# A gated mix of attention and SwiGLU on one core: GpSimd takes strips of any width, the gate's operand is made earlier, and the order table is another

## The chip, the core and the metric

The kernel runs on one core of a Trainium2 chip. The core has TensorE (matrix products, PE in the profile; its weight loads are PEld), VectorE (DVE), ScalarE (ACT) and GpSimd (POOL), and SyncE (SP), which here only issues DMAs. Matrix products go to PSUM, from where VectorE or ScalarE take them to SBUF. The metric is the device time of one execution in microseconds, as a median of several runs.

## What is computed

```python
x = A_x                                   # 2048 rows of 512, bf16
g = _sigmoid((x * gate_w).sum(-1, keepdims=True))
a = _A_ref(x, A_wqkv, A_wo)               # attention, 32 heads of 16
b = _B_ref(x, B_w_gate, B_w_up, B_w_down) # (silu(x @ w_gate) * (x @ w_up)) @ w_down, width 1792
return g * a + (1 - g) * b
```

In the attention, scores are `q k^T / 4`, the softmax runs over all 2048 keys, and its result times `v` goes through the projection `wo`. The largest part of the work is the softmax's exponentials: 32 heads x 2048 queries x 2048 keys.

## The kernel before

**Units.** Heads are taken four at a time (8 groups), queries 512 at a time (4 blocks). A pair of group and query block is a *unit*; there are 32, taken in a fixed order (`UNIT`). A unit has 16 blocks of 128 keys. For each block of keys TensorE makes scores for four heads (four tiles of 128 x 512 in PSUM), an engine takes the exponential, and TensorE multiplies the result with the values and adds it into the unit's output `o_ps`. A column of ones in the values gives the denominators. When all blocks of a unit are in, an output copy (`post`) takes `o_ps` to `osb`.

**Two ways to the exponential.** Scores that ScalarE handles go two heads at a time to `s_t` (128 x 1024 in PSUM, two buffers), and one `Exp` of ScalarE writes `e_t`; a block of keys is two such instructions. Scores that VectorE handles go one head at a time to `d_t` (128 x 512 in PSUM, three banks, shared with all other products). VectorE scales and shifts each into a 16-bit integer whose bits are a bf16 near the exponential; four of them fill a buffer of 128 x 2048 (`c_t`, or space of `kaug` or `wd_t`: NS = 7 buffers in all). The accuracy comes from a mean over shifted versions. With `groups[n] == 4`, three more *copies* are made, each the buffer plus a constant (`SHIFTS`), and TensorE multiplies all four with the values. With `groups[n] == 2`, two bit-masked copies are made and one of them becomes the *product* of the buffer with it; TensorE multiplies two versions. Copies and products are objects of class `Pass` in the list `vops`. They read and write SBUF alone.

**GpSimd's part.** GpSimd can't take PSUM here; it takes passes from VectorE: shifting copies (of groups of four) as two halves of 1024 columns (`g_half`, `GHALF`), and of products up to a few pieces of 448 columns off the end (`piece`, `G_COLS`), the rest being done by VectorE (`product`). `claim` chooses the pass, and `g_now` gives it to GpSimd if VectorE has PSUM reads ahead (`d_wait`, `owed`) that last about as long as the strip. `beside` makes the strip wait for VectorE's last SBUF operation. In the plan, `plan.lock` keeps VectorE from SBUF operations until the strip ends; on the chip no wait stands for that, only the order of the instructions on VectorE.

**The order.** The whole program is put in order by a planner in the kernel's Python: it keeps a clock per engine (`plan.pe`, `plan.dve`, `plan.act`, `plan.pool`) with a fixed cost for each kind of instruction, and decides step by step what TensorE does next (a pair of score tiles, a value product, a piece of a chain of another product) and what VectorE does next (`fill_dve`). Every instruction is chained to the one before on its engine, so the order on the engines is the planner's. `v_unit` and `v_take` decide which blocks of keys go to VectorE; `quad` whether as group of four or two. The string `TURNS` has two characters for each pair of score tiles, which change single decisions there: `turn_of` (for instance `s`: no chain piece now; `d`: no `d_t` now) and `way_of` (for instance `t`: GpSimd takes no products; `q`: a strip may end later; `n`: no strip; `f`, `g`: kind of group). A dot changes nothing.

**Around it.** The remaining products run as chains of pieces with deadlines (`Pacer`): projections, the feed-forward part (`gu`, tanh on ScalarE, `dps`, `ops`), and the normalisation. Three places matter here. `gate_end` computes the gate from `ge`, and `turn_odds`, some thirty us later in the profile, transposes it by a product with an fp32 copy `rd` of the identity, made on VectorE at the head of `turn_odds`. Unit 0 begins with a provisional bound; `q0_again` lets ScalarE compute a `ratio`, and `parts` multiplies it in by a product `rp` on TensorE. At the end, four output tiles `a_l_a`, `a_l_b`, `al`, `al_o` collect the last projection (`last_pieces` for the first two, `tail` one matmul at a time for the others), the last output copy on ScalarE gives denominators (`dt`), their reciprocals `rt` are spread by `rps`, and the last matmul of each tile follows.

Of the kernel before, what the change touches and what calls it, by code (L numbers as in the profile page):

```python
# [53 lines left out]
class Pacer:  # L54
# [33 lines left out]
    "..............h.............d...............h.............j..n....b.h.........k....ns........x.."  # L88
    ".......................y.n.......m..........s..............w......s..x........d.....b.kg...f...."
    ".........fbt....bt..b.........a.................o.......s.........s...h.dx....o................."  # L90
    "........bve..m.........wk...............s.......h.dx......i..q....h.............s...c...s......."
    "....k..g...l....o................................v.....x.f..............o.............s..v...f.."
    "................c......g..a...h..l...l...wey...wh..y....j...c....t..k...s........f....en....b..."
    "d...................a.....c......f.......................m........k..............g........c....."
    "...f...........v......dx......................sl.v.......v..j..............q..........b........."
    "..j.................s.........i.........hf.......g............................................o."
    ".............g......................h...............................................b..........."
    ".....l................................................c............x...........................g"
    "..i...i..m..e.....hm.....we.....a..xel.......v.f........o.............................h........."
    "...g..........d.s..mc.......h............................................m......................"  # L100
    ".............................................g............d......................x............s."
    "............a..v..................b.....................k"
# [4 lines left out]
def kernel(  # L107
# [771 lines left out]
    class Pass:  # L879


        def __init__(self, cost, key, n, ready, home, k, h, y):
            self.cost, self.key, self.n, self.ready, self.home = cost, key, n, ready, home
            self.k, self.h, self.y = k, h, y
            self.halves, self.c, self.left = [0, 1], None, NV * QBW

        def run(self, engine, cols=slice(0, NV * QBW), t=None):

            n, k, y = self.n, self.k, self.y
            if not self.home:  # L890
                product(n, self.h, y, self.left)
                return None
# [12 lines left out]
        def done(self, t):  # L905

            n, k, (h, c) = self.n, self.k, self.c
# [14 lines left out]
            if not todo[n]:  # L922
                vops.insert(0, Pass(MUL_US, None, n, late.pop(n) + PRODUCT_LAG, False, None, self.h, self.y))

# [12 lines left out]
    PRODUCT_LAG = 0.0  # L937
    late = {}
    todo = {}
    gq = []  # L940
    GHALF = NV * QBW // 2

    def g_half(engine, start=0.0):

        g = gq[0]
        half = g.halves.pop(0)
        ins = g.run(engine, slice(half * GHALF, (half + 1) * GHALF))
        if engine is gps:
            beside(ins)
            t = plan.pool = plan.lock = start + G_US  # L950
        else:
            t = plan.dve
        if not g.halves:
            gq.pop(0)
            g.done(t)

# [6 lines left out]
    G_US = 1.06  # L963
    G_COLS, GP_US = 448, 1.05
    G_KEEP = 2
    G_OVER = 0.1

    def claim(now):

        if gq:  # L970
            return gq[0]
        front = [v for v in vops if v.n == vops[0].n and v.poolable()] if vops else []
        if front and not front[-1].home and (front[-1].left < G_KEEP * G_COLS or way_of(pairs[0]) == "t"):
            return None
        if front and front[-1].home and min(c_free) > now + 0.05:
            return None
        return front[-1] if front and front[0].n // KT <= closed + AHEAD else None

    def g_now(now):

        while True:
            g = claim(now)
            if g is None:
                return
            start = max(plan.pool, plan.alone + 0.17, g.ready + 0.17, 0.0 if g.c is not None or not g.home else min(c_free) + 0.1)
            t = now
            for ready, cost in sorted([(d[0], 0.6) for d in d_wait] + [(o[0], o[1]) for o in owed if not wide(o[1])]):
                if ready > t + 0.05:
                    break
# [3 lines left out]
            if not g.home:  # L993
                g.piece(start)
                continue
            if not gq:
                vops.remove(g)
                gq.append(g)
            g_half(gps, start)

    def g_dve():
        if gq[0].c is None:
            plan.dve = max(plan.dve, min(c_free))
        spend_v(0.335, plan.lock)
        g_half(vec)
        took()

    def product(n, h, y, left):
        i, c = part.pop(n)
        cols = slice(0, left)  # L1010
        vec.tensor_tensor(out=c[:, cols].bitcast(BF16), in0=y[:, cols].bitcast(BF16), in1=c[:, cols].bitcast(BF16), op=ALU.mult)
        ready(n, 1, i, c)
        drop(h, plan.dve + 0.2)
        y_live[0] -= 1

    def c_ready():
        return min(c_free) if not vops or vops[0].home else vops[0].ready
# [6 lines left out]
    def pay_v():  # L1024
        v = vops.pop(0)
        spend_v(v.cost, max(plan.lock, v.ready), v.key)
        v.run(vec)
        if v.home:
            v.done(plan.dve)
        took()  # L1030

    def fill_dve():

        code = way_of(pairs[0])
        while plan.dve <= plan.pe + 0.2:
# [6 lines left out]
            fit = bool(vops) and not shut and vops[0].n // KT <= closed + AHEAD and c_ready() <= now  # L1042
# [14 lines left out]
            elif gq and not shut and gq[0].n // KT <= closed + AHEAD and (gq[0].c is not None or min(c_free) <= now):  # L1057
                g_dve()
            elif d_wait or owed or vops and vops[0].n // KT <= closed + AHEAD:
                t = min([w[0] for w in d_wait] + [max(o[0], plan.lock if wide(o[1]) else 0.0) for o in owed[:1]]  # L1060
                        + [max(c_ready(), plan.lock)] * bool(vops and vops[0].n // KT <= closed + AHEAD))
# [83 lines left out]
    def post(un):  # L1145
# [5 lines left out]
        elif un == UNITS - 1:  # L1151
            act(out=osbs[un][:, :], in_=o_of.pop(un)[:, :], func=ACT.Identity, bias=tiny[:, 0:1], scale=1.0)
# [192 lines left out]
    def q0_again(p):  # L1345
# [12 lines left out]
    def scale_part(p):  # L1358
        def f():
# [11 lines left out]
                     cond=lambda: part_done and ratio_done)  # L1371
# [228 lines left out]
    def next_pv():  # L1600
        flush_act()
        while not pv_list(None):
# [4 lines left out]
            elif gq and (gq[0].c is not None or min(c_free) < 1e9):  # L1607
                g_dve()
# [56 lines left out]
    GQL = lambda: [v for v in vops + gq if v.poolable()]  # L1665
# [77 lines left out]
    while closed < UNITS or vops or vcur or gq:  # L1743
# [26 lines left out]
    assert not vops and not gq and not vready and not vcur and not d_wait and not copies and au == closed == UNITS  # L1770
# [5 lines left out]
    tail(2)  # L1776
# [4 lines left out]
    tail(2)  # L1781
# [51 lines left out]
```

## Time and profile before

| | us |
|---|---|
| median of 3 runs | 750.89 (750.66 to 751.36) |
| the profiled execution | 751.05 |
| its span, first to last instruction | 749.1 |
| busy: TensorE, VectorE, ScalarE, GpSimd | 725.0, 726.5, 732.7, 228.3 |
| exponentials on ScalarE, 758 | 708.2 |
| reads of `d_t` on VectorE, 532 | 349.2 |
| first exponential starts, last one ends | 13.1, 740.6 |

A row of a group reads: line, engine, operation, output <- input with shape and type, count | busy us, mean ns of one | idle us before them and what ended it. Instructions overlap, so a mean is longer than the distance between starts. The helper that chains all instructions is line 191 for TensorE, 194 for ScalarE and 203 for the others; rows are told apart by their tiles. The 349.2 are the sum of the rows of `c_t`, `kaug` and `wd_t` out of `d_t` (296.3, 50.2 and 2.7).

### The profile page before, as it was taken

The numbers are of one execution on the slowest core, as the hardware profiler recorded it, in microseconds if no ns is written. First come the engines' busy times: TensorE is split into PE (matmuls) and PEld (weight loads), VectorE is DVE, ScalarE is ACT, GpSimd is POOL, SyncE is SP. The second block draws the span as 40 slices with busy tenths as digits, with TensorE's granted clock in tenths as the row PEclk, the third lists the DMA queues.
The fourth block names the chain that finished last, engine by engine and source line by source line (L and its number), as shares of the span: only waits on it lengthen the run. The fifth ranks groups of instructions, "written<-read, shape, count | busy, mean of one in ns | idle before, by whom it ended". The sixth has DMA issues, their size and how long they took to land.

```text
span 749.1 us, 22678 instructions
## 1 busy us (share of the span) xinstructions
PE 725.0 (97%) x9180; PEld 214.4 (29%) x9181; DVE 726.5 (97%) x1222; ACT 732.7 (98%) x827; POOL 228.3 (30%) x235
## 2 busy tenths in 40 slices
PE   8999999999999999999999999999999999999997
PEld 3322222223222222222222222222222222222222
DVE  6799999999999999999999999999999999999995
ACT  5999999999999999999999999999999999999996
POOL 5024323232232224242413142333232233243410
PEclk9999999999999999999999999999999999999999
DMA  8002303144210022221100231211000322100001
GB/s 197 2 1 55 74 12 73 36 123 90 59 34 13 17 52 68 61 48 30 38 19 19 52 83 35 65 35 43 17 16 27 76 68 55 34 21 12 15 29 36
DMA packets 91025, 34.43 MB, mean 46 GB/s; under 512 B 75488, under 2 KB 90472, under 8 KB 90920
## 3 DMA queue, kind: packets, MB, share of 16 engines
q1 hardware_dynamic: 89192, 32.66, 18.2%
q8 instruction: 71, 1.16, 0.6%
q10 hardware_dynamic: 1728, 0.33, 0.2%
q14 instruction: 34, 0.28, 0.1%
HBM read 21.55 MB, written 2.35 MB: 32 GB/s over the span
## 4 chain that ended last, share of the span: by engine, by line
PE 52%; ACT 31%; DVE 10%; issue 7%; ACTq 0%; DVEq 0%
ACT e_t L194 29%; PE s_t L191 17%; PE o_ps L191 15%; PE gu L191 8%; DVE c_t L203 6%; PE ops L191 6%; ACT th L194 1%; PE qp L191 1%; PE kp L191 1%; DVE mt L203 1%; PE dps L191 1%; PE vp L191 1%; PE warm L191 1%; DVE kaug L203 1%; PE d_t L191 1%
## 5 line engine op out<-in xcount | busy, mean ns | idle before, releaser
L194 ACT ACTIVATE e_t<-s_t 128x1024 bf16<-128x1024 f32 x758 | 708.2, 1087 | 2.6 <-PE s_t L191 1.4
L203 DVE TENSOR_SCALAR c_t<-d_t 128x512 uint16<-128x512 f32 x452 | 296.3, 685 | 2.1 <-PE d_t L191 1.8
L191 PE MATMUL s_t<-qx,kaug 32*128 32x512 bf16 (+1 forms) x1192 | 231.9, 384 | 9.7 <-ACT e_t L194 8.6
L191 PEld LDWEIGHTS <-kaug 32*128 32x128 bf16 (+1 forms) x2048 | 81.3, 91 | 313.2 <-issue 309.9
L203 POOL TENSOR_SCALAR c_t<-c_t 128x1024 uint16<-128x1024 uint16 x98 | 102.3, 1044 | 171.7 <-DVE c_t L203 112.7
L191 PE MATMUL d_t<-qx,kaug 32*128 32x512 bf16 x440 | 153.7, 383 | 0.0
L191 PE MATMUL o_ps<-e_t,vaug 128*32 128x512 bf16 (+2 forms) x1560 | 147.6, 380 | 0.1
L203 DVE TENSOR_SCALAR c_t<-c_t 128x2048 uint16<-128x2048 uint16 x184 | 124.3, 687 | 1.1 <-DVE c_t L203 0.5
L191 PE MATMUL o_ps<-c_t,vaug 128*32 128x512 bf16 (+2 forms) x1416 | 123.5, 369 | 0.7 <-DVE osb L203 0.5
L203 POOL TENSOR_TENSOR c_t<-c_t 128x448 bf16<-128x448 bf16 x53 | 54.2, 1034 | 173.3 <-DVE c_t L203 114.2
L191 PEld LDWEIGHTS <-vaug 128*32 128x32 bf16 x3184 | 68.5, 95 | 102.2 <-issue 88.8
L191 PE MATMUL gu<-xT,wg 128*32 128x512 bf16 x896 | 73.2, 384 | 0.0
L191 PE MATMUL gu<-xT,wu 128*32 128x512 bf16 x896 | 67.8, 382 | 0.0
L191 PE MATMUL ops<-wd_t,mt 128*32 128x512 bf16 x672 | 57.7, 382 | 0.0
L203 DVE TENSOR_TENSOR c_t<-c_t 128x1600 bf16<-128x1600 bf16 (+3 forms) x56 | 55.9, 998 | 0.0
L203 DVE TENSOR_SCALAR kaug<-d_t 128x512 uint16<-128x512 f32 x76 | 50.2, 684 | 0.2 <-PE d_t L191 0.2
L191 PE MATMUL s_t<-q,kaug 64*128 64x512 bf16 (+1 forms) x192 | 37.4, 385 | 2.8 <-ACT e_t L194 2.7
L203 DVE SCALAR_TENSOR_TENSOR mt<-gs,gu 128x512 bf16<-128x512 bf16 x56 | 38.2, 683 | 1.1
L203 DVE SCALAR_TENSOR_TENSOR gs<-th,gu 128x512 bf16<-128x512 bf16 x56 | 38.2, 682 | 0.1
L194 ACT ACTIVATE th<-gu 128x512 bf16<-128x512 f32 x56 | 37.4, 667 | 0.0
L203 POOL TENSOR_SCALAR kaug<-c_t 128x1024 uint16<-128x1024 uint16 x18 | 18.8, 1044 | 53.8 <-DVE c_t L203 42.9
L191 PEld LDWEIGHTS <-mt 128*32 128x32 bf16 (+1 forms) x1037 | 24.6, 95 | 29.1 <-issue 22.7
(148 smaller groups left out, 533.8 us busy)
## 6 DMA issues: line engine op xcount, KB each, us to landing
wg<-in_B_w_gate_dram SPq DMA_DIRECT2D x56, 128.0 KB
wu<-in_B_w_up_dram SPq DMA_DIRECT2D x56, 128.0 KB
on<-osb SPq DMA_DIRECT2D x120, 16.0 KB
rb<-rr SPq DMA_DIRECT2D x15, 128.0 KB
wd_t<-in_B_w_down_dram SPq DMA_DIRECT2D x7, 256.0 KB
qx<-qst SPq DMA_DIRECT2D x96, 16.0 KB
qx<-aq SPq DMA_DIRECT2D x96, 16.0 KB
out_dram<-o_t SPq DMA_DIRECT2D x12, 128.0 KB
```

What stands on the lines that cost most here:

```text
L191: return ordered(nc.tensor.matmul(*args, **kw))
L194: ordered(nc.scalar.activation(*args, **kw))
L203: return lambda *a, **kw: ordered(f(*a, **kw))
```

## The change

- A pass is no longer given to GpSimd in halves or pieces of 448. `strip` computes how many columns fit into the time that is left beside VectorE's PSUM reads, with a fixed part and a price per column (`G_FIX`, `G_COPY`, `G_PRODUCT`), rounds down to a multiple of 32, takes at least 192 columns and leaves either none or at least 160. VectorE does what is left of the pass, and may be left nothing. A strip is planned to start 0.10 us after VectorE's last SBUF operation instead of 0.17, and to end at most 0.05 us (was 0.1) after VectorE's PSUM reads.
- `claim` looks through the passes of the first block of keys that GpSimd can help with; two new characters (`r`, `u`) change whether VectorE takes masked copies or others first, and whether it leaves those to GpSimd.
- The fp32 identity is made in `gate_end`; `turn_odds` uses it.
- The product with `ratio` waits in the plan until ScalarE is done with it.
- The last output copy is split into halves of 256 columns, on VectorE and ScalarE.
- The matmuls of the last projection are given one at a time, where TensorE would wait for an exponential and no value product is ready, instead of three at one place.
- `TURNS` is another string (1456 characters, 1400 before).

Counted in the two programs: 756 exponentials (758 before), 536 reads of `d_t` (532), on VectorE 262 copies and 75 products (255 and 76), on GpSimd 246 copies and 81 products (138 and 72).

```diff
 TURNS = (
...
-        later(0.5, end, plan.act + 0.05)
+            rd = work.tile([P, QBW], BF16, tag="rd", name="rd")[:, :].bitcast(F32)
+            vec.tensor_copy(out=rd[:, 0:P], in_=ident[:, :])
+            odds_rows.append(rd)
+        later(1.7, end, plan.act + 0.05)
 
     def turn_odds():
-        rd = work.tile([P, QBW], BF16, tag="rd", name="rd")[:, :].bitcast(F32)
-        vec.tensor_copy(out=rd[:, 0:P], in_=ident[:, :])
+        rd = odds_rows.pop()
...
-        def piece(self, start):
-            cols = slice(self.left - G_COLS, self.left)
-            h, c = part[self.n]
-            beside(gps.tensor_tensor(out=c[:, cols].bitcast(BF16), in0=self.y[:, cols].bitcast(BF16),
-                                     in1=c[:, cols].bitcast(BF16), op=ALU.mult))
-            plan.pool = plan.lock = start + GP_US
-            self.left -= G_COLS
-            self.cost = 0.06 + (MUL_US - 0.06) * self.left / (NV * QBW)
+        def strip(self, start, us):
+            rate = G_COPY if self.home else G_PRODUCT
+            w = int((us - G_FIX) / rate) // 32 * 32
+            if self.left - w < G_LEAVE:
+                w = self.left if w >= self.left else self.left - G_LEAVE
+            if w < G_LEAST:
+                return False
+            beside(self.run(gps, slice(self.left - w, self.left)))
+            plan.pool = plan.lock = start + G_FIX + rate * w
+            self.left -= w
+            self.cost = 0.066 + ((0.6 if self.home else MUL_US) - 0.066) * self.left / (NV * QBW)
+            if not self.left:
+                vops.remove(self)
+                self.done(plan.pool)
+            return True
...
-    G_US = 1.06
-    G_COLS, GP_US = 448, 1.05
-    G_KEEP = 2
-    G_OVER = 0.1
+    G_FIX, G_COPY, G_PRODUCT = 0.195, 0.00083, 0.00187
+    G_LEAST, G_LEAVE = 192, 160
+    G_OVER = 0.05
+    MASKS = False
...
-            start = max(plan.pool, plan.alone + 0.17, g.ready + 0.17, 0.0 if g.c is not None or not g.home else min(c_free) + 0.1)
+            start = max(plan.pool, plan.alone + 0.1, g.ready + 0.1, 0.0 if g.c is not None or not g.home else min(c_free) + 0.1)
...
-            if t == now or t < start + (G_US if g.home else GP_US) - (G_OVER if way_of(pairs[0]) != "q" else 0.4):
+            if t == now or not g.strip(start, t + (G_OVER if way_of(pairs[0]) != "q" else 0.4) - start):
                 return
...
+            if vops and vops[0].poolable() and (code == "r") != MASKS:
+                j = next((j for j, v in enumerate(vops) if not v.poolable() and v.n // KT <= closed + AHEAD), 0)
+                vops.insert(0, vops.pop(j))
...
-            act(out=osbs[un][:, :], in_=o_of.pop(un)[:, :], func=ACT.Identity, bias=tiny[:, 0:1], scale=1.0)
+            o, hw = o_of.pop(un), QBW // 2
+            vec.tensor_scalar(out=osbs[un][:, 0:hw], in0=o[:, 0:hw], scalar1=tiny[:, 0:1], scalar2=None, op0=ALU.add)
+            act(out=osbs[un][:, hw:], in_=o[:, hw:], func=ACT.Identity, bias=tiny[:, 0:1], scale=1.0)
...
-            ratio_done.append(0)
+            ratio_done.append(plan.act + 0.1)
...
-                     cond=lambda: part_done and ratio_done)
+                     cond=lambda: part_done and ratio_done and ratio_done[0] <= plan.pe)
...
-            tail(3)
+        if len(a_ps) > 2 and not pv_list(plan.pe) and not vops and len(rest) > 1:
+            n = closed * KT + done_a[closed]
+            if plan.pe + 0.22 < max(e_end.get(b, 0.0) for b in range(4 * n, 4 * n + 4)):
+                tail(1)
+                spend("F", 1)
+                continue
```

More of the change, by code (lines that the diff above doesn't have):

```diff
@@ L87 @@
 TURNS = (
[L88 to L97, printed above, removed]
@@ L884, in __init__, with run @@
             self.k, self.h, self.y = k, h, y
-            self.halves, self.c, self.left = [0, 1], None, NV * QBW
-        def run(self, engine, cols=slice(0, NV * QBW), t=None):
+            self.c, self.left = None, NV * QBW
+        def run(self, engine, cols):
             n, k, y = self.n, self.k, self.y
             if not self.home:
-                product(n, self.h, y, self.left)
-                return None
+                c = part[n][1]
+                return engine.tensor_tensor(out=c[:, cols].bitcast(BF16), in0=y[:, cols].bitcast(BF16),
+                                            in1=c[:, cols].bitcast(BF16), op=ALU.mult)
             if self.c is None:
@@ L905, in done @@
         def done(self, t):
-            n, k, (h, c) = self.n, self.k, self.c
+            n, k = self.n, self.k
+            if not self.home:
+                i, c = part.pop(n)
+                copies[n, 1] = (c.bitcast(BF16), i)
+                usable(t + 0.3, n, 1)
+                drop(self.h, t + 0.2)
+                y_live[0] -= 1
+                return
+            h, c = self.c
             todo[n] -= 1
@@ L922, in done @@
             if not todo[n]:
-                vops.insert(0, Pass(MUL_US, None, n, late.pop(n) + PRODUCT_LAG, False, None, self.h, self.y))
+                vops.insert(0, Pass(MUL_US, None, n, late.pop(n), False, None, self.h, self.y))
         def poolable(self):
             return not self.home or groups[self.n] == 4
-        def piece(self, start):
-            cols = slice(self.left - G_COLS, self.left)
-            h, c = part[self.n]
-            beside(gps.tensor_tensor(out=c[:, cols].bitcast(BF16), in0=self.y[:, cols].bitcast(BF16),
-                                     in1=c[:, cols].bitcast(BF16), op=ALU.mult))
-            plan.pool = plan.lock = start + GP_US
-            self.left -= G_COLS
-            self.cost = 0.06 + (MUL_US - 0.06) * self.left / (NV * QBW)
-    PRODUCT_LAG = 0.0
+        def strip(self, start, us):
[13 more added lines that the diff above has]
+            return True
     late = {}
     todo = {}
[L940 to L955, printed above, removed]
     def beside(ins):
@@ L961, in beside @@
                               reason="beside reads of PSUM")
-    G_US = 1.06
-    G_COLS, GP_US = 448, 1.05
-    G_KEEP = 2
-    G_OVER = 0.1
+    G_FIX, G_COPY, G_PRODUCT = 0.195, 0.00083, 0.00187
+    G_LEAST, G_LEAVE = 192, 160
+    G_OVER = 0.05
+    MASKS = False
     def claim(now):
[L970 to L977, printed above, removed]
+        first = next((v.n for v in vops if v.poolable() and v.n // KT <= closed + AHEAD), None)
+        front = [v for v in vops if v.n == first and v.poolable() and (v.c is not None or not v.home or min(c_free) <= now + 0.05)]
+        if way_of(pairs[0]) == "t":
+            front = [v for v in front if v.home]
+        begun = [v for v in front if v.left < NV * QBW]
+        return (begun or front or [None])[-1]
     def g_now(now):
@@ L990, in g_now @@
                 t += cost
-            if t == now or t < start + (G_US if g.home else GP_US) - (G_OVER if way_of(pairs[0]) != "q" else 0.4):
+            if t == now or not g.strip(start, t + (G_OVER if way_of(pairs[0]) != "q" else 0.4) - start):
                 return
[L993 to L1014, printed above, removed]
     def c_ready():
-        return min(c_free) if not vops or vops[0].home else vops[0].ready
+        return min(c_free) if not vops or vops[0].home and vops[0].c is None else vops[0].ready
     def pay_d():
@@ L1664 @@
     EAGER = lambda q, b: q == 0 and b <= 4
-    GQL = lambda: [v for v in vops + gq if v.poolable()]
+    GQL = lambda: [v for v in vops if v.home and v.poolable()]
     back = [0]
@@ L1742 @@
     flush_act()
-    while closed < UNITS or vops or vcur or gq:
+    while closed < UNITS or vops or vcur:
         fill_dve()
@@ L1769 @@
         pay()
-    assert not vops and not gq and not vready and not vcur and not d_wait and not copies and au == closed == UNITS
+    assert not vops and not vready and not vcur and not d_wait and not copies and au == closed == UNITS
     assert not at
@@ L1775 @@
     osb = osbs[un]
-    tail(2)
+    tail(min(2, len(rest)))
     dt = m_tile("dt")
```

38 lines of the change are left out of this document (22 added, 16 removed).

## The prediction

> **What bounds the kernel now.** I read the busy line of the page first, then the costly groups, then the waits, then the timeline around single stalls.
>
> ```profile
> PE 725.0 (97%) x9180; PEld 214.4 (29%) x9181; DVE 726.5 (97%) x1222; ACT 732.7 (98%) x827; POOL 228.3 (30%) x235
> ...
> L194 ACT ACTIVATE e_t<-s_t 128x1024 bf16<-128x1024 f32 x758 | 708.2, 1087 | 2.6 <-PE s_t L191 1.4
> L203 DVE TENSOR_SCALAR c_t<-d_t 128x512 uint16<-128x512 f32 x452 | 296.3, 685 | 2.1 <-PE d_t L191 1.8
> ```
>
> Three engines are busy 97 to 98%, so the average decides nothing. Idle is 16 to 24 us each, nearly all before 40 us and after 740 us; in the middle, the table by stretches has this:
>
> ```profile
> 200.00:300.00 100.00, 96.92 (x1243) 27.59 (x1235) 99.18 (x162) 99.04 (x112) 31.26 (x30) 1.00 0.16 40
> 500.00:600.00 100.00, 99.75 (x1299) 28.03 (x1297) 99.72 (x164) 100.00 (x113) 32.39 (x32) 1.00 0.14 34
> ```
>
> (Columns after the length: PE, PEld, DVE, ACT, POOL, clock, DMA share, GB/s.) So I count steps from start to start. ScalarE:
>
> ```profile
> 727.67 12.95 ACT L194 ACTIVATE e_t<-s_t 128x1024 bf16<-128x1024 f32 x14
> 118.38 0.62 ACT L194 ACTIVATE th<-gu 128x512 bf16<-128x512 f32 x1
> 118.86 6.56 ACT L194 ACTIVATE e_t<-s_t 128x1024 bf16<-128x1024 f32 x7
> ```
>
> Fourteen exponentials: (12.95 - 1.087) / 13 = 0.9125 us a step; a tanh 118.86 - 118.38 = 0.48. From the first exponential (13.11) to the end of the last (740.61) are 727.5 us. 758 x 0.9125 + 56 x 0.48 + 0.6 (two small ones) + 0.2 (the last one's end) = 719.4. ScalarE loses 8.1 us there, mostly in slips too short to show as idle. VectorE, by the same method (0.60 a step for a 512-column PSUM read or a 2048-column copy: 221.05 to 221.65; 1.13 for a whole product: 221.65 to 222.78), has 669.9 us of work between the first and the 31st output copy (at 44.5 and 721.5, 677.0 us), each instruction that stands between them at its step; ScalarE has 669.3 for the score tiles and gates issued there. These two are the bound, equally. TensorE has about 645 by the steps below, and waits for ScalarE (11.9 us in the table of waits).
>
> **The change part by part.** The two programs were counted instruction by instruction.
>
> Exponentials 758 to 756: one more block of keys goes to VectorE (a block is two exponentials, or four reads of d_t with what follows). ScalarE: -2 x 0.9125 = -1.83 us, on the path.
>
> VectorE: d_t reads 532 to 536, +2.4 us. Copies 255 with 520,192 columns become 262 with 492,960. The by-form rows give 687 ns at 2048 columns and 422 at 1024, 0.259 ns a column; less the overlap of 0.09 the rest is 0.07 an instruction: +0.5 - 7.0 = -6.5. Products 76 with 123,392 columns become 75 with 118,432; rows 1219 ns at 2048, 986 at 1600, 751 at 1152 give 0.523 a column: -2.7. Sum -6.8 us of 670, one of the two bounds.
>
> GpSimd: 138 copies of 1024 columns (1.044) and 72 products of 448 (1.034), 218.5 us, become 246 copies with 172,640 columns and 81 products with 39,264. The trace has one width of each, so the fixed part of a strip is not in it. Lower bound: the small memset's 0.10 (128x4), 274 us in all; upper: the 128x128 select's 0.29, 287 us. The planner's new 0.195 lies between and reproduces both known widths (0.195 + 0.85 = 1.045; 0.195 + 0.838 = 1.033); I take it: 280 us, so POOL's busy time goes to about 290 (284 to 297). GpSimd itself stays far from full. What it costs is on VectorE, and is bounded next.
>
> Strips against VectorE's SBUF work. The planner now assumes a strip to start 0.10 after VectorE's last SBUF operation (0.17 before), and fills VectorE's stretch of PSUM reads up to 0.05 beyond its end. Of about 160 strips that began right behind such an operation, 54 started 0.07 to 0.09 after its recorded end, 103 at 0.13 to 0.19, and a recorded end is itself some 0.09 after the next start. So strips will end about 0.08 later against the plan than now. Does that hold VectorE? Two rows:
>
> ```profile
> 331.14 1.05 POOL L203 TENSOR_SCALAR c_t<-c_t 128x1024 uint16<-128x1024 uint16 x1 [1.68 <-PE d_t L191]
> 332.06 0.69 DVE L203 TENSOR_SCALAR c_t<-c_t 128x2048 uint16<-128x2048 uint16 x1
> ...
> 199.98 2.17 POOL L203 TENSOR_SCALAR c_t<-c_t 128x1024 uint16<-128x1024 uint16 x2 [2.63 <-DVE c_t L203]
> 201.51 0.72 DVE L203 CAST rd<-ident 128x128 f32<-128x128 bf16 x1
> ```
>
> The copy at 332.06 starts 0.13 before the strip's end and takes its usual 0.69; 48 operations start 0.02 to 0.13 early and none is stretched. The cast at 201.51, 0.64 before the end, lasts until just after it: 0.72, for 128 columns. So an overlap up to 0.13 is free and a long one is held. The new overlap should be about 0.10 to 0.21. Lower bound of the cost: 0. Upper: half of 327 strips (48 of 210 now, but strips cut to a single 0.60 read will more often be followed by a copy) x 0.08 = 13 us on VectorE. I take 4, nearer the free rows, which leaves VectorE -6.8 + 4 = -2.8, still no worse than ScalarE's -1.8. The Trainium skill, SBUF — State Buffer, section "SBUF: two separate sides", says that the port pair shared by VectorE and GpSimd is an exclusive lock held for the whole instruction. By that rule every overlap would cost its length and the cost would be the upper bound or more; the cast agrees, the 48 rows do not up to 0.13.
>
> TensorE: two score rounds fewer, two 512-column rounds more (one value product, one filler), and 16 more switches between row and column tiling. From the chain (score step 0.32, then 0.33 for the first column group and 0.22 for each further) two switches cost 0.65 - 2 x 0.217 = 0.22: 8 x 0.22 = +1.7 us. I take nothing of it, since 11.9 us of waits for ScalarE cover it; uncovered, it is 1.7.
>
> The gate's fp32 operand. Now:
>
> ```profile
> 202.28 0.28 PE L191 MATMUL odds_p<-rd,odds 128*16 128x128 f32 x1 [1.17 <-DVE rd L203]
> 203.31 1.94 ACT L194 ACTIVATE e_t<-s_t 128x1024 bf16<-128x1024 f32 x2 [0.81 <-PE d_t L191]
> ```
>
> TensorE stands 1.17 for the cast that the strip held; the score tiles behind it are late and ScalarE idles 0.81. With the cast made some thirty us earlier this goes: -0.81. The cast itself stays on VectorE, at 0.2 to 0.7, in the 4 above.
>
> The ratio's condition. In the waits TensorE stands 1.03 us for ScalarE's ratio at 31.7; the exponentials there start at 31.48 and 32.74, 1.26 apart where 0.91 is usual: -0.35. Late next could be the deadline of that chain; its result is wanted only by the first output copy at 44.5.
>
> The end. The last output copy in halves on two engines: ScalarE 687 ns at 512 columns and 1087 at 1024 is 0.78 a column, 0.49 for 256; VectorE, with 742 at 512, is taken to need no longer for its half; -0.20. Now three matmuls of the last projection stand between the last score tile and the last two value products; the new order puts three column groups of another chain and four row matmuls there (0.65 + 0.43 + 0.1 against 0.65 + 0.75 now, with the same last score), so the last products can follow the exponential: -0.45. The three matmuls are made behind the reciprocals instead: 3 x 0.217 = +0.65. Together 0.0; I take 0, with -0.5 and +0.7 as ends.
>
> Sum: -1.83 - 0.81 - 0.35 + 0.0 = -3.0. The profiled execution has a span of 749.1 and a time of 751.05 (1.95 around it), 0.16 above the median of the three runs. Span 746.1, time 748.05; against the median 747.9.
>
> **The rivals.** (a) Slower: the strips hold VectorE. If the free overlap ends at 0.13 and half the strips overrun by 0.06, VectorE pays 160 x 0.06 = 9.6, net +2.8, and as the other bound it carries the end: 753.7. It decides from 6.8 / 327 = 0.021 us a strip on, where the relief is eaten. For it: two thirds of the strips start late already; a pair of strips takes 2.17, 0.08 more than two singles, which the plan leaves out. Against it: the 48 rows. (b) Faster still: of ScalarE's 8.1 us of slips 1.2 is accounted for above. If the other 6.9 comes from tiles that VectorE returns late, and 6.8 us less work there halves it, the time is 747.9 - 3.4 = 744.5. Against it: the taken 4 us of holds, and more dependences across three engines. (c) No change: TensorE paces. The chain gives it 52% and ScalarE 31%; then +1.7 stands against the -1.16 of the two stalls and the exponentials gain nothing: 750.9 + 0.5 = 751.4. Against it: its 645 us of steps to 670.
>
> **How the numbers follow.** My forecast has 0.51 (its own range 746.3 to 749.4), (b) 0.15, (c) 0.14, (a) 0.20. A difference of 0.2%, 1.5 us, is about what a measurement can tell. Faster, below 749.4: 0.51 + 0.15 = 0.66; within: 0.14; slower, above 752.4: 0.20. Range: from (b)'s value to most of (a)'s, 744.3 to 753.2, which leaves out some 0.04 below and 0.12 above.
>
> **What would show it.** Right: 756 exponentials at 0.91 to 0.93 a step, the wait of odds_p and that of rp gone, VectorE's busy time some 3 to 7 us lower, POOL near 290. Strips of 416 columns at 0.54 confirm the price; at 0.60 the fixed part is nearer 0.29 and the holds grow. Wrong by (a): 2048-column copies or narrow remainders on VectorE with means well over 687 ns, and more ScalarE idle in the middle. Wrong by (c): ScalarE's idle or mean step grows while TensorE has no waits for it.

## The result, and the profile after

| | before | after |
|---|---|---|
| median, us | 751.12 (750.34 to 751.99) | 754.48 (753.69 to 754.78) |
| profiled execution, its span | 751.05, 749.1 | 753.96, 752.2 |
| up to the first output copy | 44.5 | 42.8 |
| from there to the 31st output copy | 677.0 | 682.3 |
| from there to the end | 27.5 | 27.1 |

The ratio is 1.0042, with an interval of 1.0029 to 1.0055: slower by 0.42%, where 747.9 us was forecast. The three stretches of the span say where: the start gained 1.7 us, the end 0.4, and the middle, 30 units of the same work, lost 5.3. Of the start's 1.7 only 1.5 lie behind the first exponential; when that one starts differs by up to 1.1 us between executions of one order (12.6 to 13.7 in the runs below).

The page's busy line and two of its costly groups, after the change:

```profile
PE 731.6 (97%) x9213; PEld 215.6 (29%) x9213; DVE 728.6 (97%) x1233; ACT 733.4 (98%) x825; POOL 291.9 (39%) x352
...
L195 ACT ACTIVATE e_t<-s_t 128x1024 bf16<-128x1024 f32 x756 | 707.7, 1071 | 4.5 <-PE d_t L192 1.7
L204 DVE TENSOR_SCALAR c_t<-d_t 128x512 uint16<-128x512 f32 x460 | 299.7, 679 | 2.1 <-PE d_t L192 1.8
```

VectorE was to have 6.8 us less work, 2.8 us less with the holds that I allowed for. It is busy 2.1 us longer (726.5 before). TensorE, with 33 instructions more, is busy 6.6 us longer, and the exponentials' mean has fallen from 1087 to 1071: steps are shorter than recorded durations, so these hold some overlap with the instruction ahead, and I read a lower mean as score tiles that come too late for it.

The groups of VectorE with shapes kept apart, before and then after, show what has grown (the columns: count, busy us and mean ns):

```profile
L203 DVE TENSOR_SCALAR c_t<-c_t 128x2048 uint16<-128x2048 uint16 x184 | 124.3, 687 | 1.1 <-DVE c_t L203 0.5
L203 DVE TENSOR_TENSOR rn<-rd 128x128 bf16<-128x128 f32 x3 | 1.0, 344 | 0.1
L203 DVE TENSOR_TENSOR omg<-ge,gval 128x16 f32<-128x16 f32 x1 | 0.2, 174 | 0.0
```

```profile
L204 DVE TENSOR_SCALAR c_t<-c_t 128x2048 uint16<-128x2048 uint16 x165 | 114.0, 698 | 0.3
L204 DVE TENSOR_SCALAR c_t<-kaug 128x2048 uint16<-128x2048 uint16 x30 | 20.8, 705 | 0.1
L204 DVE TENSOR_TENSOR rn<-rd 128x128 bf16<-128x128 f32 x3 | 2.3, 773 | 0.1
L204 DVE TENSOR_TENSOR omg<-ge,gval 128x16 f32<-128x16 f32 x1 | 1.0, 962 | 0.0
```

The same whole copies take 698 and 705 on average instead of 687, and a few small operations several times as long. The timeline of after shows two such places (start, duration, instruction):

```profile
605.50 1.80 POOL L204 TENSOR_SCALAR kaug<-c_t 128x1120 uint16<-128x1120 uint16 x2 [2.99 <-DVE c_t L204]
...
606.45 0.68 DVE L204 TENSOR_SCALAR c_t<-d_t 128x512 uint16<-128x512 f32 x1
...
607.05 0.80 DVE L204 TENSOR_SCALAR c_t<-c_t 128x2048 uint16<-128x2048 uint16 x1
```

```profile
171.11 2.15 POOL L204 TENSOR_SCALAR kaug<-c_t 128x800 uint16<-128x800 uint16 x2
...
172.03 0.25 DVE L204 RECIPROCAL gval<-omg 128x16 f32<-128x16 f32 x1
...
172.32 0.96 DVE L204 TENSOR_TENSOR omg<-ge,gval 128x16 f32<-128x16 f32 x1
```

At 607.05 a copy of 2048 columns starts 0.25 us before a pair of strips ends (605.50 + 1.80 = 607.30), and takes 0.80 instead of 0.69. At 172.32 an operation of 16 columns starts 0.94 before the end of such a pair (173.26) and lasts until 173.28. The reciprocal between them, at 172.03, lies wholly beside the same strips and takes its usual 0.25.

On VectorE the changed kernel has the same sequence of instructions whether its strips are wide or narrow, so their durations can be set side by side with those of a run with narrow strips (the third experiment). In after 63 instructions are longer there by more than 0.02 us, together by **8.8 us**. The ten longest make 4.8 of it, the other 53 make 4.0. In before, against its own version with narrow strips, two are longer, by 0.65 together; one is the cast that the prediction showed.

### The profile page after: what moved, and what is told of

It is laid out like the page before. It is cut to its first block, busy times and chain, and to the rows that moved or that the text cites. A ratio compares the mean times of both kernels' runs of the same rounds, so it can differ in the third digit from the quotient of the medians.

```text
span 752.2 us, 22877 instructions
## 1 busy us (share of the span) xinstructions
PE 731.6 (97%) x9213; PEld 215.6 (29%) x9213; DVE 728.6 (97%) x1233; ACT 733.4 (98%) x825; POOL 291.9 (39%) x352
## 4 chain that ended last, share of the span: by engine, by line
PE 57%; DVE 22%; ACT 14%; issue 5%; POOL 1%; DMA 0%; DVEq 0%; ACTq 0%; POOLq 0%
PE s_t L192 19%; PE o_ps L192 17%; DVE c_t L204 14%; ACT e_t L195 13%; PE gu L192 7%; PE ops L192 5%; PE qp L192 2%; PE kp L192 2%; PE vp L192 2%; DVE mt L204 2%; DVE kaug L204 2%; ACT th L195 1%; DVE gs L204 1%; DVE osb L204 1%; PE dps L192 1%
## 5 line engine op out<-in xcount | busy, mean ns | idle before, releaser
L195 ACT ACTIVATE e_t<-s_t 128x1024 bf16<-128x1024 f32 x756 | 707.7, 1071 | 4.5 <-PE d_t L192 1.7
L204 DVE TENSOR_SCALAR c_t<-d_t 128x512 uint16<-128x512 f32 x460 | 299.7, 679 | 2.1 <-PE d_t L192 1.8
L204 POOL TENSOR_SCALAR c_t<-c_t 128x416 uint16<-128x416 uint16 (+19 forms) x173 | 136.6, 789 | 208.4 <-DVE c_t L204 154.8
L192 PEld LDWEIGHTS <-kaug 32*128 32x128 bf16 (+1 forms) x2048 | 79.3, 91 | 304.9 <-issue 301.6
L204 DVE TENSOR_SCALAR c_t<-c_t 128x2048 uint16<-128x2048 uint16 (+3 forms) x187 | 121.8, 662 | 0.3
L204 POOL TENSOR_TENSOR c_t<-c_t 128x480 bf16<-128x480 bf16 (+13 forms) x60 | 65.2, 1103 | 131.9 <-DVE c_t L204 84.5
L204 DVE TENSOR_TENSOR c_t<-c_t 128x2048 bf16<-128x2048 bf16 (+15 forms) x57 | 56.9, 998 | 0.0
L204 DVE TENSOR_SCALAR kaug<-d_t 128x512 uint16<-128x512 f32 x72 | 47.0, 680 | 0.6 <-PE d_t L192 0.6
L192 PE MATMUL s_t<-q,kaug 32*128 32x512 bf16 (+1 forms) x188 | 36.6, 385 | 1.1 <-ACT e_t L195 0.9
L204 POOL TENSOR_SCALAR kaug<-c_t 128x416 uint16<-128x416 uint16 (+15 forms) x34 | 26.8, 788 | 22.2 <-DVE c_t L204 20.0
L204 POOL TENSOR_SCALAR c_t<-kaug 128x1120 uint16<-128x1120 uint16 (+8 forms) x33 | 24.8, 753 | 23.1 <-DVE c_t L204 13.8
```

The costliest lines, as they stand in the source:

```text
L192: return ordered(nc.tensor.matmul(*args, **kw))
L195: ordered(nc.scalar.activation(*args, **kw))
L204: return lambda *a, **kw: ordered(f(*a, **kw))
```

## The experiments

Two theories stood against each other. A: the holds explain the loss; GpSimd's strips end too late for VectorE's next SBUF operation, which is stretched. B: the new order itself is worse, and the holds lie beside other work. Each diff is against the kernel named; ratios are to the kernel before.

**Fixed buffers (e1).** In the next two runs the strips leave columns of a buffer unwritten. For that the six pass buffers are made once and filled once, instead of being taken anew for each pass. This run has only that, in the changed kernel:

```diff
+    homes = [vex.tile([P, NV * QBW], U16, tag=f"h{i}", name="c_t", bufs=1) for i in range(NS - 1)]
+    for h in homes:
+        nc.gpsimd.memset(h[:, :].bitcast(F32), 1.0)
...
-            return i, vex.tile([P, NV * QBW], U16, tag=f"h{i}", name="c_t", bufs=1)[:, :]
+            return i, homes[i][:, :]
```

> The changed kernel with the six buffers of the passes made once and filled once by GpSimd at the start (before its first strip), instead of being made anew for each use. Nothing is left out, and the order on TensorE, VectorE and ScalarE is the same. It is the footing of the two kernels that shorten strips. Every theory: no change against the changed kernel, 753.5 to 755.5 us.

Measured: 754.99, ratio 1.0057 (1.0042 to 1.0072); the middle 683.5, VectorE's lengthening 10.4. That is within the measurement's uncertainty of the changed kernel, and it is what the next two are compared with.

**Strips a little shorter (e2).** The planner's decisions stay, and so does the order on VectorE, TensorE and ScalarE; each strip just ends earlier, by 96 columns of a copy or 64 of a product (by the strip's price per column, 0.08 and 0.12 us).

```diff
-            beside(self.run(gps, slice(self.left - w, self.left)))
+            short = 96 if self.home else 64
+            beside(self.run(gps, slice(self.left - w, self.left - short)))
```

> As e1_fixed_buffers, with each strip of GpSimd shorter by 96 columns (copies, 0.08 us by 0.83 ns a column) or 64 (products, 0.12 us); nobody computes these columns, so part of the exponentials is left out and stale numbers take their place. The order and VectorE's own instructions are the same. Theory A (strips that overrun hold VectorE's SBUF operations; the trace of the changed kernel shows about 8.6 us of stretched instructions there against 0.7 before): the short overlaps of 0.15 to 0.3 us go, most of the stretch with them, 749 to 751.5 us. Theory B (the new order itself is slower, the stretch fills idle time): 753.5 to 755 us.

Measured: 750.04, ratio 0.9989 (0.998 to 0.9998). The middle is 677.9, 5.6 less than with full strips (683.5 in e1); the lengthening is 2.6 instead of 10.4, in 10 instructions instead of 73. A tenth of a microsecond at the end of each strip decides whether the kernel is slower or slightly faster than before.

**Strips of 32 columns (e3).**

```diff
-            beside(self.run(gps, slice(self.left - w, self.left)))
+            beside(self.run(gps, slice(self.left - 32, self.left)))
```

> As e1_fixed_buffers, with every strip cut to 32 columns; the other columns of a strip are left out (stale numbers in their place). Same order. Theory A: also the long overlaps go, VectorE has no stretched instruction left, and the time falls to what the order gives without interference: 746 to 749.5 us, by the forecast's sum of ScalarE and the tail. Theory B: 753 us or more.

Measured: 748.04, ratio 0.9963 (0.995 to 0.9976); span 746.3, middle 676.6. Its busy line, and the place that was shown of after at 605 to 607 us:

```profile
PE 725.2 (97%) x9212; PEld 214.4 (29%) x9213; DVE 721.9 (97%) x1233; ACT 730.5 (98%) x825; POOL 88.2 (12%) x358
```

```profile
601.30 0.50 POOL L204 TENSOR_SCALAR kaug<-c_t 128x32 uint16<-128x32 uint16 x2 [3.84 <-DVE c_t L204]
...
602.25 0.69 DVE L204 TENSOR_SCALAR c_t<-d_t 128x512 uint16<-128x512 f32 x1
...
602.85 0.69 DVE L204 TENSOR_SCALAR c_t<-c_t 128x2048 uint16<-128x2048 uint16 x1
```

The copy behind the strips takes 0.69. With no interference from GpSimd the new order is faster than the kernel before, by about what was forecast without the holds. That rejects B, unless the old order gains as much by the same edit.

**The kernel before with strips of 32 columns (e4).** The same for before, with the fixed buffers:

```diff
-            cols = slice(self.left - G_COLS, self.left)
+            cols = slice(self.left - 32, self.left)
...
-        ins = g.run(engine, slice(half * GHALF, (half + 1) * GHALF))
+        ins = g.run(engine, slice(half * GHALF, half * GHALF + (32 if engine is gps else GHALF)))
```

> The kernel before with fixed buffers and every piece given to GpSimd cut to 32 columns, the other columns left out (stale numbers). Same order as before. Both theories: its strips held VectorE only 0.7 us in all, nearly all of it the cast that delayed the gate's transpose, so 749 to 751 us. Against e3_strips_tiny it says which of the two orders is the better one without GpSimd: by theory A the new one by 1 to 4 us, by theory B the old one by 2 or more.

Measured: 750.52, ratio 0.9993 (0.9983 to 1.0003), POOL busy 62.6. The old order had next to nothing to gain. Between the two orders without GpSimd's work lie 750.52 - 748.04 = 2.5 us in favour of the new one; GpSimd's full strips then cost the new one 6.4 to 7.0 us (754.48 or 754.99 less 748.04) and the old one 0.6, too little to tell from nothing. B falls: the strips cost the time, not the order. A has one reservation: shorter strips take away everything that strips do to the other engines, not the holds of VectorE alone. A second way by which they cost time is shown further below.

**The kernel before with longer halves (e7).** If the end of the strips is all there is to it, the old order can be made slow in the same way. GpSimd's halves of a copy are 1216 columns instead of 1024, overlapping the other half by 192, so that the planner's times for them are exceeded by about 0.16 us:

```diff
-        ins = g.run(engine, slice(half * GHALF, (half + 1) * GHALF))
+        more = 192 if engine is gps else 0
+        ins = g.run(engine, slice(half * (GHALF - more), half * (GHALF - more) + GHALF + more))
```

> The kernel before with each half copy of GpSimd lengthened by 192 columns beyond the middle (1216 instead of 1024), so that some columns are computed twice with the same result; nothing is left out, VectorE's instructions and the order are the same. A strip lasts 0.16 us longer (1216 columns at 0.83 ns), the second of two in a row ends 0.32 later. Theory A (overruns beyond 0.15 us hold VectorE, and each us held costs 0.7 us of time): overlaps of 0.02 to 0.13 become 0.18 to 0.29 and more, 5 to 9 us of stretch, 754 to 757 us. Theory B (the new order, not the overruns, made the changed kernel slower): 750.5 to 752 us.

Measured: 757.2, ratio 1.0076 (1.0061 to 1.0091); the middle 683.3 instead of 677.0; 58 lengthened instructions with 6.9 us together instead of 2 with 0.65. One of them:

```profile
337.88 1.21 POOL L203 TENSOR_SCALAR c_t<-c_t 128x1216 uint16<-128x1216 uint16 x1
...
338.75 0.88 DVE L203 TENSOR_SCALAR c_t<-c_t 128x2048 uint16<-128x2048 uint16 x1
```

An overlap of 0.34 (338.75 to 339.09), 0.19 longer. The stretch grew by 6.2 us for 6.3 us of added holds. Not all of it came by the holds: from 86.30 to 93.95 six lengthened halves follow each other on GpSimd, TensorE waits 0.60 for the last of them at 93.99, and the exponentials are 1.0 later from there on (timelines of e7 and of before).

**The operand alone (e6).** The one part that I could price from a single row, made in the kernel before:

```diff
             vec.reciprocal(odds[:, :], ge[:, :])
+            rd = work.tile([P, QBW], BF16, tag="rd", name="rd")[:, :].bitcast(F32)
+            vec.tensor_copy(out=rd[:, 0:P], in_=ident[:, :])
+            odds_rows.append(rd)
...
-        rd = work.tile([P, QBW], BF16, tag="rd", name="rd")[:, :].bitcast(F32)
-        vec.tensor_copy(out=rd[:, 0:P], in_=ident[:, :])
+        rd = odds_rows.pop()
```

> The kernel before with one part of the change alone: the fp32 identity is made in gate_end; the planner's costs are left as they were, so the order of everything else is the same. Forecast of that part: TensorE's wait of 1.17 us at odds_p goes, ScalarE's idle of 0.81 with it, 0.8 us less: 750.2 to 750.6. Rival: the slack behind it takes the gain, 751.0.

Measured: 750.22, ratio 0.9988 (0.9979 to 0.9996); the middle 676.26, 0.77 less than before (677.03). In its timeline TensorE no longer waits for the cast, and four exponentials follow each other in 3.88 without a pause:

```profile
200.16 3.88 ACT L194 ACTIVATE e_t<-s_t 128x1024 bf16<-128x1024 f32 x4
...
201.78 0.28 PE L191 MATMUL odds_p<-rd,odds 128*16 128x128 f32 x1
```

This is the fastest complete kernel of the study, ahead of both.

**The last output copy whole (e5),** in the changed kernel:

```diff
-            o, hw = o_of.pop(un), QBW // 2
-            vec.tensor_scalar(out=osbs[un][:, 0:hw], in0=o[:, 0:hw], scalar1=tiny[:, 0:1], scalar2=None, op0=ALU.add)
-            act(out=osbs[un][:, hw:], in_=o[:, hw:], func=ACT.Identity, bias=tiny[:, 0:1], scale=1.0)
+            act(out=osbs[un][:, :], in_=o_of.pop(un)[:, :], func=ACT.Identity, bias=tiny[:, 0:1], scale=1.0)
```

> The changed kernel with the last output copy made in one piece by ScalarE, as before; the rest is the changed kernel and the order is its own. In the changed kernel ScalarE's half waited 1.03 us and started only when VectorE's half had ended, so the two take 743.75 to 744.73 instead of one 0.69. Theory A (the halves follow each other and the split costs): the stretch from the end of the last exponential to the end of the span shrinks by 0.2 to 0.4 us from 8.96, time 754.0 to 754.5. Theory B (the split gains 0.2, as forecast, and something else made the tail longer): it grows by 0.2.

Measured: 754.42, ratio 1.0043 (1.0029 to 1.0056). The time can't tell it from the changed kernel. In the traces the stretch from the end of the last exponential to the end of the span is 8.74, against 9.00 with the halves (the expectation's 8.96 goes by rounded ends) and 8.44 before. The timeline of after has the reason:

```profile
743.75 0.48 DVE L204 TENSOR_SCALAR osb<-o_ps,tiny 128x256 bf16<-128x256 f32 x1 [0.33 <-PE o_ps L192]
...
744.26 0.47 ACT L195 ACTIVATE osb<-o_ps,tiny 128x256 bf16<-128x256 f32 x1 [1.03 <-DVE osb L204]
```

The halves run one after the other: ScalarE waits for VectorE's write to the same tile. 0.99 us from the first start to the last end, where the whole copy took 0.69.

**The new code with the old table (e8).** The changed kernel with `TURNS` of the kernel before (the strings have 1401 characters there and 1473 in the changed kernel):

```diff
 TURNS = (
-    "....d...sq.t.......q................i......v...........ld..q...........y........................"
...
+    "..............h.............d...............h.............j..n....b.h.........k....ns........x.."
...
 )
```

> The changed kernel's code with the table of the kernel before. The order is another one throughout, made for neither. If the table is worth little, 753 to 756 us, as with the new table; if an order must be chosen for its code, some us to 10 us more, 757 to 766.

Measured: 762.07, ratio 1.0143 (1.0124 to 1.0161). Its busy line:

```profile
PE 735.0 (97%) x9272; PEld 219.1 (29%) x9273; DVE 716.3 (94%) x1222; ACT 740.7 (97%) x835; POOL 230.0 (30%) x285
```

With this table the planner gives VectorE less (94% busy) and ScalarE 766 exponentials, eight more than before; eight steps of 0.9125 are 7.3 of the 10.9 us. The old string marks single places of the old order, and in another order its letters meet other places. So table and strips can't be costed apart by swapping the string, and this run says nothing on the holds.

## Why the prediction was wrong

**The step that failed** is "I take 4, nearer the free rows", the price of holding VectorE, with what follows from it there: that VectorE stays "no worse than ScalarE's -1.8", so that the sum has nothing for the holds. They measured 8.8, inside the bounds of 0 and 13, and close to the 9.6 of rival (a), whose mechanism this is in the main (753.7 forecast for it, 754.48 measured). How close is luck: the rival had 160 holds of 0.06, and there are 63 of 0.14 on average. Sorted by how far an SBUF operation of VectorE's starts before the recorded end of a strip, after the change, the operations are:

| overlap, us | operations | mean lengthening, us |
|---|---|---|
| up to 0.13 | 55 | -0.01 |
| 0.13 to 0.16 | 10 | 0.005 |
| 0.16 to 0.20 | 33 | 0.024 |
| 0.20 to 0.25 | 16 | 0.083 |
| 0.25 to 0.30 | 17 | 0.116 |
| 0.30 to 0.50 | 6 | 0.18 |
| over 0.50 | 12 | 0.31 |

The 48 rows that I called free were free: where VectorE was held, the lengthening is the overlap less about 0.15. Eight of the 18 operations in the last two rows were not held at all (two reductions, a reciprocal, one operation beside a memset, a cast, and three copies beside which the strip was the longer one); the other ten were, by 0.23 to 0.79. In before the copies and products overlapped by 0.13 at most, just below that limit, and the new plan moved them across it. I had forecast overlaps of "about 0.10 to 0.21"; 98 of the 149 lie below 0.20, but 51 lie above, and these carry nearly all of the cost. The trace of after has two reasons. Half of the strips still began late: of 160 that directly followed an operation of VectorE's, alone or as the first of a row, 77 started 0.06 to 0.10 us behind its recorded end and 83 at 0.14 to 0.19. The plan now counts 0.10 from its own end of that operation; the recorded end lies some 0.09 later, so the plan has every strip start 0.01 behind the recorded end, earlier than either group. The old 0.17 stood for 0.08, the early group. And copies that follow each other on GpSimd lose 0.06 to 0.08 between one and the next, which the plan leaves out, as the prediction said of pairs: at 119 places, 34 before. Of 44 single strips with an early start none ended more than 0.20 after the start of VectorE's next SBUF operation, of 40 single ones with a late start 7, and of 76 rows of two or more 30. The reading that was missing was the limit: I knew that 0.13 was free and put a single price on everything beyond, with the weight on the side where the rows were, though the change was to leave that side.

Some of it I had not priced at all. The four longest holds are `omg` (0.79), two of the three `rn` (0.75 and 0.69) and the product of `on` with `rb` (0.63), 2.9 us together. The function `g_now` adds up the work beside which a strip may run, and counts every owed operation with a cost of 0.45 or more as work on PSUM; `gate_end` at 1.7 and `spread` at 0.87 or 1.1 pass that test, but part of what they issue reads and writes SBUF, `omg` and `rn` among it. The product of `on` with `rb` has a cost of 0.345 and doesn't pass; its strip, at 616.55, is the fifth of a row that began at 612.10. My upper bound of 13 was half the strips by 0.08 each and had no term for such an operation.

The Trainium skill, SBUF — State Buffer, section "SBUF: two separate sides", says that the shared pair of ports is taken by whichever starts first, for the whole instruction, and that on VectorE's side it concerns operations in a two-port mode or with two SBUF inputs (these only against a GpSimd operation that reads SBUF). This trace agrees on the kinds: 303 operations that read PSUM ran beside strips and none was longer by over 0.011 us, nor were reciprocals; copies, the products and, in before, a cast were. Which one waits does not follow from the recorded starts: the strips at 713.27, 715.37 and 717.22 have recorded starts 0.37, 0.07 and 0.01 us ahead of VectorE's copies, and it was the strips that took longer. The prediction took only the sentence on the lock from it and set the 48 free rows against it. What measurement adds is the 0.15 us before the recorded end in which an overlap costs nothing.

**A wait that I had not thought of** is the other way round. Late in the program seven strips follow each other, and three of them were held by VectorE's copies. They are on the chain that ended last, and TensorE waits for the fifth:

```profile
713.27 1.44 POOL L204 TENSOR_SCALAR c_t<-c_t 128x416 uint16<-128x416 uint16 x1 [0.62 <-DVE c_t L204]
...
713.64 0.68 DVE L204 TENSOR_SCALAR c_t<-c_t 128x2048 uint16<-128x2048 uint16 x1
...
718.28 0.40 PE L192 MATMUL o_ps<-c_t,vaug 128*32 128x512 bf16 x4 [0.81 <-POOL c_t L204]
```

From here on the exponentials are 1.0 us later, set against e2 or e3, where that wait is missing. So of the 5.7 us that the middle lost against e3, about 1.0 came by GpSimd's own lateness and 4.6 by the holds of VectorE. I had written that "GpSimd itself stays far from full" and left it out.

**The relief of 6.8 us of VectorE's work** was counted rightly, but spread over the whole program. In the middle, the only stretch where VectorE is a bound, its work by steps went from 669.9 to 666.3, 3.6 less. The rest lies in the first and the last unit. So even holds of 4 would have left VectorE no better than before (-3.6 + 4 = +0.4). With the measured holds it is -3.6 + 8.8 = +5.2, and the stretch measured +5.3, but this agreement is an accident: without holds (e3) the relief of 3.6 made the middle only 0.4 shorter, and not every us of a hold reaches the end. Between e1 and e2 5.0 of 7.8 us did, between e2 and e3 2.0 of 2.6, in the old order 6.06 of 6.27 (e7); less the 1.0 that came by TensorE's wait for a strip, in the first and in the last, these are about 0.5, 0.76 and 0.8 us per us.

**ScalarE's two exponentials** left, but not from the middle. In the three stretches 33, 705 and 20 start before, 32, 705 and 19 after and in e3. The gain of 1.83 was real as a term of the sum and lies in the first stretch and behind the 31st copy.

**The two stalls** went. The wait of `odds_p` (1.17) is gone in after and in e6, where it alone is worth 0.8 in the middle and 0.9 in the medians, for 0.81 forecast. The wait for the ratio is gone too, and the 23 exponentials from 31.72 us on take 0.912 a step. The forecast counted one long step there, 0.35; the timeline of before has three, 1.26, 1.20 and 1.03 from 31.48 on, 0.75 in all.

**The tail** was forecast at 0.0 with ends of -0.5 and +0.7, and is +0.56. Its terms: the halves +0.30 instead of -0.20, because they are serialised (this I had not seen as possible); the earlier last products -0.35 for -0.45 (from the last exponential's end to the copy 0.86 before, 0.51 after); behind the copy +0.60, which holds the three matmuls that were to cost +0.65.

**The cover of TensorE** is not settled. Rival (c) has 751.4, and e3, with all of TensorE's work, 748.04: its number is out. But without GpSimd's work the middle is as long in the new order as in the old (676.6 in e3, 676.5 in e4), though VectorE has 3.6 less to do there; whether TensorE's 1.7 us of switches took some of that, no run shows. In after TensorE carries more of the chain, 57% against 52%, but in e3 too, 58%; what came with the strips is the share of VectorE, 22% against 10% before and 11% in e3:

```profile
PE 57%; DVE 22%; ACT 14%; issue 5%; POOL 1%; DMA 0%; DVEq 0%; ACTq 0%; POOLq 0%
```

**The price of a strip** was right: 0.195 fixed, and the widths that the trace of before lacked come out at it. The groups of after, with shapes kept apart, for 416 and 1120 columns of a copy and 480 of a product (planned 540, 1125 and 1093 ns):

```profile
L204 POOL TENSOR_SCALAR c_t<-kaug 128x416 uint16<-128x416 uint16 x8 | 4.3, 537 | 4.2 <-DVE c_t L204 2.1 <-PE d_t L192 0.9 <-PE gu L192 0.8
L204 POOL TENSOR_SCALAR c_t<-kaug 128x1120 uint16<-128x1120 uint16 x8 | 9.0, 1123 | 13.8 <-DVE c_t L204 7.5 <-PE d_t L192 4.7 <-DVE kaug L204 1.5
L204 POOL TENSOR_TENSOR c_t<-c_t 128x480 bf16<-128x480 bf16 x24 | 26.3, 1095 | 77.9 <-DVE c_t L204 54.6 <-PE d_t L192 16.4 <-PE qp L192 4.2
```

POOL is busy 291.9, forecast 290. I had written that strips "at 0.54 confirm the price", with larger holds only at 0.60. So this sign pointed the wrong way: the duration of a strip was planned to a hundredth, its start was not.

Without the holds my terms give a span of 746.1 and a time of 748.05; e3 has 746.3 and 748.04. The agreement is in good part luck. The middle gained 0.4 instead of 0.81, and the tail was off by 0.56; the ratio's wait gave 0.4 more than forecast, and the first exponential started 0.5 earlier, which is within what executions of one order differ by. The step from there to 754.48 is GpSimd's strips, shown by taking their work away (e2, e3) and by lengthening them in the other order (e7): the holds in the main, and the wait at 718.28 with about 1.0. How the two share it is read from the traces, and no run separates them.

What stays open: why a strip starts either 0.08 or 0.16 us behind the operation it waits for, and what holds the middle of e3 where it is. No experiment asked for either, and a version of the new order planned with the later start and with `omg` and `rn` kept out of the strips' cover was not run.

## What to carry to other kernels

When work goes to an engine that shares a resource with the bound engine, price the end of each piece, not its length: find in the trace how much overlap is free (here 0.15 us), how far the present pieces are from that limit, and what the change does to that distance, with the time lost between pieces that follow each other. That no operation was stretched among pieces that all lie inside the limit says nothing about pieces outside. And count a saving only in the stretch where its engine is the bound; the small change with one visible wait behind it (e6, -0.12%) was worth more than the large one.

## What the runs showed of the hardware

- VectorE's operations that read PSUM, and its reciprocals, ran beside a GpSimd operation at full speed here: at most 0.011 us longer in 303 cases for the first, and none for the second in overlaps of up to 1.6 us. Next to a reciprocal of 16 columns at its usual 0.25 us a product of 16 columns took 0.96 for 0.17 (timeline at 172).
- It goes the other way as well. In six places of after the strip was the longer one: a copy of 416 columns that takes 0.54 alone took 1.44 beside VectorE's whole copy at 713.64, which kept its 0.68. The six make 2.5 us on GpSimd; 2.0 of it, in a row of strips that TensorE waits for, is what makes the exponentials 1.0 us later at 719. By an estimate from these rows, the three strips of that row that were lengthened end as if each had begun 0.15 before the recorded end of VectorE's copy: 713.64 + 0.68 - 0.15 + 0.54 = 714.71, and 713.27 + 1.44 = 714.71.
- The first 0.15 us or so of an overlap, counted back from the recorded end of the GpSimd operation, cost VectorE nothing (the table by overlap: 65 operations below 0.16, at most 0.005 on average).
